# Attention in full fp32 on halves of TensorE, with no hi/lo splits and TensorE in program order

## Chip, core and metric

The kernel runs on one core of one Trainium2 chip. The metric is the device time of one execution in microseconds. Before the change the median of three runs is 1240.89 us (1240.23 to 1241.39).

## Reference

Block-causal attention over 8 batches and 8 heads (576 positions, head size 64, blocks of 64) is followed by a bilinear feed-forward layer on the 4608 x 512 result.

```python
def _attn_ref(q, k, v):
    scores = (1.0 / np.sqrt(D)) * np.matmul(q, k.transpose(0, 1, 3, 2))
    mask = pos[:, None] // 64 >= pos[None, :] // 64
    scores = np.where(mask, scores, -1e9)
    scores = scores - np.max(scores, axis=-1, keepdims=True)
    attn = np.exp(scores)
    attn = attn / (np.sum(attn, axis=-1, keepdims=True) + 1e-09)
    return np.matmul(attn, v).astype(np.float32)

x = attn_out.transpose(0, 2, 1, 3).reshape(B * S, H * D)      # 4608 x 512
return ((x @ w_a) * (x @ w_b)) @ w_out                         # 512 -> 1536 -> 512
```

All inputs are fp32, and so are the results. q and k are drawn about four times as wide as v.

## The kernel before, in words

**Two phases.** The first phase does the attention of 64 heads, and mixed into it the feed-forward layer for four of twelve blocks of 128 hidden units ("moe" below; helper `mm3`, line 223). The second phase (lines 746 and 792) does the other eight blocks. It starts when the matmuls of `first_pass` and its tail (`o_ahead`, line 583) are through. The change touches nothing in it.

**Number formats.** The chip takes fp32 in two ways here. An `F32` matmul is shown in the trace as two MATMUL records (two passes, each with a weight load of its own). An `F32R` matmul is one record. For F32R the kernel splits an operand into a high part and a remainder (`split`, lines 112 and 115) and adds the products. The first `NATIVE = 8` heads use F32 directly, with 64 rows of the array (head size 64); the other 56 use splits. For those, q and k are split (`split_q`, `split_k`), the parts are copied by DMA so that high and low lie in the two 64-row halves of one tile (`spread`), and one F32R matmul over 128 rows sums two products. v is split into 64 + 64 columns (`split_v`), and the attention matrix into `ah` and `al` (line 478).

**One head.** There are four tiles t = 0..3 of 128 query rows, which see 192, 320, 448 and 512 keys, and a "side" tile of 128 rows by 128 keys for the first and last block. The generators are `softmax` (scores on PE; row maxima with `top` on DVE, line 404; exponentials with `exps` on ACT, line 407; sums and reciprocal `rc`; multiplication by `rc` on POOL, line 451), `turn` (14 transposes of 128 x 128 on PE, line 474; copies `ah` out of PSUM on ACT, line 476) and `values` (products with v into `av`, copied to `xf`). PSUM has three score buffers, two buffers `tp` for the transposes and one `av`.

**Slots.** The loop at the end goes through 66 slots. In slot s, head s starts, head s-1 is transposed and head s-2 gets its values; the table `SLOT` says in which order the generators step, and how many moe matmuls come after a step (its third number, 36 in a full slot). Moe matmuls start at 10.2 slots (`MOE_FROM`) with 31 to a slot, and with 36 from slot 18 on. Until slot 11 the loop also emits the conversion of the weights (`convert_w`, five steps a slot on DVE and ACT). `KEEP` adds empty matmuls in the first slots.

**Order.** `PE_ORDER` is empty: the scheduler of the language orders the instructions of every engine, PE too, by its own estimate of when they can run.

Of the kernel before, what the change touches and what calls it, by code (L numbers as in the profile page):

```python
# [9 lines left out]
F32 = mybir.dt.float32  # L10
# [22 lines left out]
PE_ORDER = []  # L33
NATIVE = 8
SPARE = 8
WARM = 9
KEEP = {(0,3):4,(1,0):2,(1,1):2,(1,2):2,(1,3):6}
# [17 lines left out]
def attention_then_bilinear_ffn(  # L55
# [11 lines left out]
    B, H, D, S = kT.shape  # L67
    SQ = qT.shape[3]
# [216 lines left out]
    c0 = [min(max(P * c - BLK, 0), S - BLK - 256) for c in range(NCH)]  # L285
    W = S - BLK
    SIDE, SIDE_T = 3, 1
    SC = slice(P * SIDE_T, P * SIDE_T + BLK), slice(P * SIDE_T + BLK, P * (SIDE_T + 1))
    NE = 2
# [15 lines left out]
    if WARM:  # L305
        z = apool.tile([P, NCH, W], F32R, tag="al", name="z")[:, 0]
        nc.vector.memset(f32(z), 0.0)
        ps = ps_mm.tile([P, 512], F32, tag="mm", name="warm")
        for k in range(WARM):
            nc.tensor.matmul(ps, z[:, :P], z, start=True, stop=True)  # L310
# [4 lines left out]
    pairs = {}  # L315

    def load_pair(p):

        b, h = divmod(2 * p, H)
        n = f"{b}_{h}"  # L320
        if 2 * p < NATIVE:
            qp = apool.tile([P, 1, SQ], F32, tag="q2", name=f"qp{n}", bufs=3)
            kp = apool.tile([P, 2, S], F32, tag="k2", name=f"kp{n}", bufs=3)
        else:
            qp = apool.tile([P, 2, SQ], F32, tag="qp", name=f"qp{n}", bufs=2)
            kp = apool.tile([P, 2, S], F32, tag="kp", name=f"kp{n}", bufs=2)
        nc.sync.dma_start(kp[:, 1], kT[b, h:h + 2].rearrange("h d s -> (h d) s"))
        nc.sync.dma_start(qp[:, 0], qT[b, h:h + 2].rearrange("h d s -> (h d) s"))
        pairs[p] = qp, kp
        for j in range(2):  # L330
            heads[2 * p + j] = {"q": qp[j * D:(j + 1) * D, 0], "k": kp[j * D:(j + 1) * D, 1]}
# [5 lines left out]

    def split_q(p):
        qp = pairs[p][0]
        if 2 * p < NATIVE:  # L340
            nc.vector.tensor_scalar_mul(qp[:, 0], qp[:, 0], SCALE)
            return
        nc.scalar.mul(qp[:, 1].bitcast(F32R), qp[:, 0], SCALE)
        behind_of(nc.vector.scalar_tensor_tensor(
            qp[:, 0], qp[:, 0], SCALE, qp[:, 1], op0=ALU.mult, op1=ALU.subtract), "rc")

    def split_k(p):
        kp = pairs[p][1]
        if 2 * p >= NATIVE:
            nc.scalar.copy(kp[:, 0].bitcast(F32R), kp[:, 1])  # L350
            nc.gpsimd.tensor_tensor(kp[:, 1], kp[:, 1], kp[:, 0], op=ALU.subtract)

    def spread(i):

        if i < NATIVE:
            return
        qp, kp = pairs[i // 2]
        n = "%d_%d" % divmod(i, H)
        own = slice(i % 2 * D, (i % 2 + 1) * D)
        q2 = heads[i]["q2"] = apool.tile([P, SQ], F32R, tag="q2", name=f"q2{n}", bufs=3)  # L360
        k2 = heads[i]["k2"] = apool.tile([P, 2, S], F32R, tag="k2", name=f"k2{n}", bufs=3)
        for j in range(2):
            part_ = slice(j * D, (j + 1) * D)
            nc.sync.dma_start(f32(q2[part_]), qp[own, 1 - j])
            nc.sync.dma_start(f32(k2[part_]), kp[own])

    def split_v(i):

        if i < NATIVE:
            return  # L370
        n = "%d_%d" % divmod(i, H)
        vr = heads[i]["vr"]
        v2 = heads[i]["v2"] = apool.tile([P, NCH + 1, 2, D], F32R, tag="v2", name=f"v2{n}", bufs=2)
        split(v2[:, :, 0], v2[:, :, 1], vr, nc.scalar, nc.gpsimd)
# [5 lines left out]
    def softmax(i):  # L380

        t, n = heads[i], "%d_%d" % divmod(i, H)
        native = i < NATIVE
        if native:
            qm, ks = t["q"], [t["k"]]
        else:
            qm, ks = t["q2"], [t["k2"][:, j] for j in range(2)]
# [7 lines left out]
        def scores(t, ps):  # L395
            w = nk[t] if native else max(nk[t], 256)
            for i, kk in enumerate(ks):
                mark = nc.tensor.matmul(  # L398
                    ps[:, :w], qm[:, q0[t]:q0[t] + P], kk[:, :w], start=(i == 0), stop=(i == len(ks) - 1)
                )  # L400
            return mark
# [7 lines left out]

        if i < SPARE:  # L410
            ps = ps_mm.tile([P, 512], F32, tag="mm", name=f"sl{n}")
        else:
            ps = ps_sc.tile([P, 512], F32, tag="sc", name=f"sl{n}")

        p1 = ps_sc.tile([P, 512], F32, tag="sc", name=f"s1{n}")
        side = p1[:, nk[1]:nk[1] + P]
        for j, kk in enumerate(ks):
            nc.tensor.matmul(side, qm[:, q0[NT]:], ends(kk), start=(j == 0), stop=(j == len(ks) - 1))  # L418
        nc.vector.memset(side[:BLK, BLK:], NEG)
        nc.vector.memset(side[BLK:, :BLK], NEG)  # L420
        mark = scores(LAST, ps)
        top(NT, side)
        top(LAST, ps)

# [3 lines left out]
            nb[BLK:], two[BLK:, None, :].to_broadcast([P - BLK, 2, 2]), axis=AX.X, op=ALU.min)  # L428
        exps(NT, e_s, side, nb[:, 1:])
        exps(LAST, es[LAST], ps, nb[:, :1])  # L430
        yield mark
        for t in range(LAST):
            ps = p1 if t == 1 else ps_sc.tile([P, 512], F32, tag="sc", name=f"s{t}{n}")
            mark = scores(t, ps)

            nc.vector.memset(ps[:BLK, nk[t] - BLK:nk[t]], NEG)
            top(t, ps[:, :nk[t]])
            exps(t, es[t][:, :nk[t]], ps[:, :nk[t]], nm[:, t:t + 1])
            if t < LAST - 1 or not native:
                yield mark  # L440
        ins = nc.vector.tensor_reduce(rc, sm, axis=AX.X, op=ALU.add)
        if not native:
            behind_of(ins, "nb")
# [9 lines left out]
        if native:  # L453
            yield mark

    def turn(i):
# [4 lines left out]
        native = i < NATIVE  # L461
        ah = apool.tile([P, NCH, W], F32 if native else F32R, tag="ah", name=f"ah{n}")
        al = None if native else apool.tile([P, NCH, W], F32R, tag="al", name=f"al{n}")
        heads[i]["a"] = ah, al
        for t in range(LAST, -1, -1):
# [11 lines left out]
            def lower(tp=tp, m=m, cols=cols):  # L477
                return nc.vector.tensor_tensor(al[:, :m, cols], tp[:, :m], f32(ah[:, :m, cols]), op=ALU.subtract)  # L478

            if t == SIDE_T and not native:  # L480
                yield mark
                behind_of(lower(), "rc")
                continue
            if not native:
                ins = lower()
                if t == 0:
                    behind_of(ins, "rc")
            yield mark

    def values(i):  # L490
# [4 lines left out]
        ah, al = t["a"]  # L495
# [6 lines left out]
        if i < NATIVE:  # L502
            an, vr = ah, t["vr"]
            av0 = ps_t.tile([P, 512], F32, tag="tp", name=f"av0{n}", bufs=2)
            nc.tensor.matmul(av0[:D, :BLK], vr[:, NCH], an[:, SIDE, SC[0]], start=True, stop=True)
            nc.scalar.copy(xo[:, :BLK], av0[:D, :BLK])

            at = [0] + [P * c - BLK for c in range(1, NCH)] + [W - BLK, W]
            for g in range(NCH + 1):
                cols = slice(at[g], at[g + 1])  # L510
                last = min(g, NCH - 1)
                for c in range(last + 1):
                    mark = nc.tensor.matmul(  # L513
                        av[:D, cols], vr[:, c], an[:, c, cols], start=(c == 0), stop=(c == last and g < NCH)
                    )
                if g == 2:
                    yield mark
            nc.tensor.matmul(av[:D, W - BLK:], vr[:, NCH], an[:, SIDE, SC[1]], start=False, stop=True)
            nc.scalar.copy(xo[:, BLK:], av[:D])
        else:  # L520
            v2 = t["v2"]
            for c in range(NCH):
                mark = nc.tensor.matmul(av[:, c0[c]:], v2[:, c], ah[:, c, c0[c]:], start=(c == 0), stop=False)  # L523
            yield mark
            av0 = ps_t.tile([P, 512], F32, tag="tp", name=f"av0{n}", bufs=2)
            for j, a in enumerate((ah, al)):
                nc.tensor.matmul(av0[:, :P], v2[:, NCH], a[:, SIDE, SIDE_T * P:][:, :P], start=(j == 0), stop=(j == 1))
            for c in range(NCH - 1, -1, -1):
                mark = nc.tensor.matmul(av[:, c0[c]:], v2[:, c], al[:, c, c0[c]:], start=False, stop=(c == 0))  # L529

            lo = apool.tile([D, S + BLK], F32, tag="avlo", name=f"avlo{n}", bufs=1)
            lo0, lo = lo[:, :P], lo[:, P:]
            nc.scalar.copy(lo0, av0[D:, :P])
            nc.vector.tensor_tensor(xo[:, :BLK], av0[:D, :BLK], lo0[:, :BLK], op=ALU.add)
# [73 lines left out]
    for p in range(2):  # L608
        load_pair(p)
        split_q(p)  # L610
# [329 lines left out]
```

## Time and profile before

| | |
|---|---|
| median of 3 runs | 1240.89 us |
| span of the profiled execution | 1238.6 us |
| first moe matmul | 95.23 us after the span's start |
| first matmul of the second phase | 677.04 us |
| PE matmul records, busy | 7849, 1222.5 us |
| DVE, ACT, POOL busy | 974.6, 706.6, 415.5 us |

The profiled execution has no wall time of its own beside its span; the 2.3 us between the span and the median lie around the span. PE's busy time overlaps from record to record, since matmuls are pipelined; what a matmul costs is read from the distance between the starts of neighbouring records.

### The profile page before, as it was taken

How to read it: one execution, taken by the hardware profiler on the slowest of the kernel's cores; microseconds unless marked ns; L12 is line 12 of the kernel's file. 1: busy time of each engine (PE TensorE's matmuls, PEld its weight loads, DVE VectorE, ACT ScalarE, POOL GpSimd, SP SyncE). 2: the span in 40 equal slices, each digit the busy share in tenths (PEclk: the TensorE clock that was granted, in tenths of full speed). 3: DMA queues.
4: the chain of work that ended last, by engine and by line, in shares of the span. 5: the costliest groups of instructions: out<-in, count | busy, mean ns of one | idle time of the engine just before them, and what ended most of it. 6: DMA issues, size and time to landing. Idle time of an engine off the chain costs nothing.

```text
span 1238.6 us, 23305 instructions
## 1 busy us (share of the span) xinstructions
PE 1222.5 (99%) x7849; PEld 1170.0 (94%) x7849; DVE 974.6 (79%) x2485; ACT 706.6 (57%) x1770; POOL 415.5 (34%) x583
## 2 busy tenths in 40 slices
PE   9989999999999999999999999999999999999998
PEld 5668999999999999999999999999999999999998
DVE  6898888777877778778889988878878677677654
ACT  5788878788788887888756345334334222222210
POOL 4467666566665666656500022022021000000000
PEclk8999999999999999999999999999999999999999
DMA  6468766767667776676234266266298344144131
GB/s 222 140 185 224 199 161 166 188 170 185 164 172 181 176 185 164 169 182 158 71 121 150 92 152 167 82 157 162 76 258 272 122 141 127 40 140 126 28 103 64
DMA packets 86583, 187.13 MB, mean 151 GB/s; under 512 B 11200, under 2 KB 46016, under 8 KB 86464
## 3 DMA queue, kind: packets, MB, share of 16 engines
q1 hardware_dynamic: 74944, 166.76, 48.6%
q0 software_dynamic: 6912, 9.44, 4.8%
q10 hardware_dynamic: 4608, 9.44, 2.2%
q8 instruction: 63, 1.03, 0.3%
q14 instruction: 56, 0.46, 0.1%
HBM read 87.03 MB, written 47.19 MB: 108 GB/s over the span
## 4 chain that ended last, share of the span: by engine, by line
PE 85%; DVE 7%; DMA 3%; ACT 2%; issue 1%; POOL 1%; SPq 0%; ACTq 0%; DVEq 0%; POOLq 0%
PE pso_z L792 15%; PE ps L223 12%; PE psx_z L746 8%; PE psw_z L746 8%; PE psv_z L746 8%; PE tp L474 8%; PE pso L223 5%; PE s L398 5%; PE psy_z L746 4%; PE av L523 3%; PE av L529 3%; PE sl L398 2%; PE av L513 2%; PE s L418 1%; DMA kp<-kT 1%
## 5 line engine op out<-in xcount | busy, mean ns | idle before, releaser
L223 PE MATMUL ps<-xh,wab 128*128 128x288 f32 x1024 | 240.7, 303 | 0.0
L792 PE MATMUL pso_z<-h_z,wo 128*128 128x384 f32 x1152 | 203.1, 334 | 0.0
L451 POOL TENSOR_SCALAR e<-e,rc 128x512 f32<-128x512 f32 (+3 forms) x256 | 154.6, 616 | 137.7 <-DVE rc L448 122.7
L792 PEld LDWEIGHTS pso_z<-h_z,wo 128*128 128x128 f32 x1152 | 199.9, 188 | 0.4 <-ACT h_z L112 0.3
L223 PEld LDWEIGHTS ps<-xh,wab 128*128 128x128 f32 x1024 | 172.0, 188 | 3.4
L223 PE MATMUL ps<-xl,wab 128*128 128x288 f32 x512 | 154.2, 301 | 0.0
L478 DVE TENSOR_TENSOR al<-tp,ah 128x512 fp32r<-128x512 f32 x224 | 131.7, 607 | 27.7 <-ACT ah L476 26.7
L112 ACT CAST h_z<-u_z 128x384 fp32r<-128x384 f32 x96 | 49.3, 514 | 180.0 <-DVE u_z L771 163.4
L476 ACT CAST ah<-tp 128x512 fp32r<-128x512 f32 x224 | 116.7, 533 | 53.0 <-PE tp L474 49.5
L474 PE MATMUL tp<-ident,e 128*128 128x128 f32 x832 | 135.9, 278 | 5.0 <-DVE al L478 1.8
L855 POOL DMA_DIRECT2D part<-pt x48 | 42.8, 1012 | 291.4 <-ACT pt L854 291.3
L474 PEld LDWEIGHTS tp<-ident,e 128*128 128x128 f32 x832 | 100.5, 141 | 20.0 <-issue 6.7
L223 PE MATMUL pso<-hh,wo 128*128 128x288 f32 x480 | 118.6, 308 | 0.0
L746 PE MATMUL psx_z<-xh,wab 128*128 128x384 f32 x384 | 116.4, 338 | 1.8 <-DVE u_z L764 1.8
L407 ACT ACTIVATE e<-s,nm 128x192 f32<-128x192 f32 (+2 forms) x192 | 101.8, 530 | 28.3 <-DVE nm L404 18.4
L746 PE MATMUL psw_z<-xh,wab 128*128 128x384 f32 x384 | 116.2, 338 | 0.0
L746 PE MATMUL psv_z<-xh,wab 128*128 128x384 f32 x384 | 116.2, 338 | 0.0
L404 DVE TENSOR_REDUCE nm<-s 128x1 f32<-128x128 f32 (+3 forms) x256 | 109.8, 430 | 2.1
L223 PEld LDWEIGHTS ps<-xl,wab 128*128 128x128 f32 x512 | 96.4, 188 | 3.6 <-POOL xl L115 0.2
L398 PE MATMUL s<-k,q 128*128 128x256 f32 x336 | 80.7, 321 | 2.1 <-ACT e_s L407 1.6
L223 PEld LDWEIGHTS pso<-hh,wo 128*128 128x128 f32 x480 | 81.5, 189 | 1.2
L115 POOL TENSOR_TENSOR v<-vr,v 128x320 fp32r<-128x320 f32 x56 | 49.7, 887 | 91.6 <-ACT v L112 78.6
(147 smaller groups left out, 2857.9 us busy)
## 6 DMA issues: line engine op xcount, KB each, us to landing
k<-kp SPq DMA_DIRECT2D x112, 288.0 KB, 4.2
xr<-xd SPq DMA_DIRECT2D x48, 384.0 KB, 4.0
q<-qp SPq DMA_DIRECT2D x112, 160.0 KB, 2.5
raww<-wab SPq DMA_DIRECT2D x24, 512.0 KB, 3.8
qp<-qT SPq DMA_DIRECT2D x32, 320.0 KB, 3.2
vr<-vm SPq DMA_DIRECT2D x64, 160.0 KB, 3.3
kp<-kT SPq DMA_DIRECT2D x32, 288.0 KB, 3.3
xd<-xf ACTq DMA_DIRECT2D x32, 288.0 KB, 4.8
```

Of the source, the lines that this page charges most:

```text
L112: nc.scalar.copy(hi, src)
L115: return lo_eng.tensor_tensor(lo, src, f32(hi), op=ALU.subtract)
L223: mm = nc.tensor.matmul(ps, w_, d_, start=(i == 0), stop=(i == n - 1))
L398: mark = nc.tensor.matmul(ps[:, :w], qm[:, q0[t]:q0[t] + P], kk[:, :w], start=(i == 0), stop=(i == len(ks) - 1))
L404: nc.vector.tensor_reduce(nm[:, t:t + 1], view, axis=AX.X, op=ALU.max, negate=True)
L407: nc.scalar.activation(out, view, AF.Exp, bias=bias, accum_out=sm[:, t, :1])
L451: nc.gpsimd.tensor_scalar(ev, ev, rc[:, t:t + 1], 1.0, op0=ALU.mult, op1=ALU.mult)
L474: mark = nc.tensor.transpose(tp[:, c], src, ident)
L476: nc.scalar.copy(ah[:, :m, cols], tp[:, :m])
L478: return nc.vector.tensor_tensor(al[:, :m, cols], tp[:, :m], f32(ah[:, :m, cols]), op=ALU.subtract)
L746: nc.tensor.matmul(ps, wt[:, i, iw], j[:, ix], start=start and kp == 0 and i == 0 and j is xh, stop=kp == KP - 1 and i == 1, skip_group_ch ...
L792: nc.tensor.matmul(ps, wt[:, a, osl], b, start=i == 0, stop=i == 3 * len(fs) - 1)
```

## The change

All 64 heads use F32. The host gives q and k twice, so that 64 channels lie in both halves of the 128 rows. Scores of tiles 1 and 3 use rows 0 to 63, those of tiles 0, 2 and the side tile rows 64 to 127. Values go into two halves of `av`: columns 0 to 63 of the array hold the outputs for the first 384 positions, columns 64 to 127 those for the last 192. `spread`, the splits and `al` are gone. There are three sets of exponential buffers for two, `SLOT` and `KEEP` have other entries, q is scaled on POOL, and PE runs the first phase in program order; the other engines are still ordered by the scheduler.

```diff
-PE_ORDER = []
-NATIVE = 8
-SPARE = 8
+PE_ORDER = ["PE"]
-KEEP = {(0,3):4,(1,0):2,(1,1):2,(1,2):2,(1,3):6}
+KEEP = {(0, 0): 6, (1, 0): 3, (1, 1): 3, (1, 2): 2, (1, 3): 2, (1, 4): 2}
...
+    CUT = 320
-    NE = 2
+    NE = 3
...
+    def scale_q(i):
+        qq = heads[i]["q"]
+        (nc.vector if i < 2 else nc.gpsimd).tensor_scalar(qq, qq, SCALE, 1.0, op0=ALU.mult, op1=ALU.mult)
...
-    def split_q(p):
...
-    def spread(i):
...
-    def split_v(i):
...
+        def scores(out, t, half, keys):
+            rows = slice(half * D, (half + 1) * D)
+            return nc.tensor.matmul(out, qm[rows, q0[t]:q0[t] + P], keys[rows], start=True, stop=True)
...
+        ps = [ps_sc.tile([P, 512], F32, tag="sc", name=f"s{t}{n}") for t in (1, 0)][::-1]
+        side = ps[0][:, nk[0]:nk[0] + P]
+        scores(side, NT, 1, ends(kk))
+        scores(ps[1][:, :nk[1]], 1, 0, kk[:, :nk[1]])
+        mark = scores(ps[0][:, :nk[0]], 0, 1, kk[:, :nk[0]])
...
+        ps += [ps_sc.tile([P, 512], F32, tag="sc", name=f"s{t}{n}") for t in (LAST, 2)][::-1]
+        scores(ps[LAST], LAST, 0, kk[:, :nk[LAST]])
+        mark = scores(ps[2][:, :nk[2]], 2, 1, kk[:, :nk[2]])
...
-        al = None if native else apool.tile([P, NCH, W], F32R, tag="al", name=f"al{n}")
...
+        for c in range(NCH):
+            a0 = max(P * c - BLK, 0)
+            if a0 < CUT:
+                part_(slice(D), slice(BLK + a0, BLK + CUT), vr[:, c], ah[:, c, a0:CUT], c == 0, False)
+            else:
+                part_(slice(D), slice(BLK), vr[:, NCH], ah[:, SIDE, SC[0]], False, True)
+            part_(slice(D, P), slice(W - CUT), vr[:, c], ah[:, c, CUT:], c == 0, False)
+        mark = part_(slice(D, P), slice(W - CUT - BLK, W - CUT), vr[:, NCH], ah[:, SIDE, SC[1]], False, True)
+        nc.scalar.copy(xo[:, :BLK + CUT], av[:D, :BLK + CUT])
+        nc.vector.tensor_copy(xo[:, BLK + CUT:], av[D:, :W - CUT])
...
-    SLOT = [(S_, 0, 3), (S_, -1, 0), (T_, -2, 4), (S_, 0, 4), (V_, -2, 3), (S_, 0, 3),
-            (T_, -1, 4), (V_, -2, 3), (S_, 0, 3), (T_, -1, 5), (T_, -1, 4)]
+    SLOT = [(S_, 0, 0), (V_, -2, 7), (S_, -1, 0), (T_, -1, 6), (S_, 0, 7), (T_, -1, 5), (T_, -1, 5), (T_, -1, 6)]
```

**PE, the start of a steady slot.** Here batch 3's head 4 starts (`s13_4` holds tile 1 and the side tile, `sl3_4` tile 3, `s03_4` tile 0), and head 2 gets its values; `x2` is the split's two matmuls. Before:

```order
L418 MATMUL s13_4_3981<-k23_4_3768,q23_4_3767 128x128 x2
L398 MATMUL sl3_4_3980<-k23_4_3768,q23_4_3767 128x512 x2
L223 MATMUL ps0_2_0_1_3997<-xh2_0_0_2651,wab1_80 128x288
...
L398 MATMUL s03_4_4022<-k23_4_3768,q23_4_3767 128x256 x2
...
L523 MATMUL av3_2_4033<-ah3_2_3897,v23_2_3854 128x512
L523 MATMUL av3_2_4033<-ah3_2_3897,v23_2_3854 128x448
L523 MATMUL av3_2_4033<-ah3_2_3897,v23_2_3854 128x320
L523 MATMUL av3_2_4033<-ah3_2_3897,v23_2_3854 128x256
L398 MATMUL s13_4_3981<-k23_4_3768,q23_4_3767 128x320 x2
```

The same place now, one head later (head 5 starts, head 3 gets its values; each row is one F32 matmul of two passes; `128x` rows are scores, `64x` rows values):

```order
L350 MATMUL s03_5_3600<-k3_5_3190,q3_5_3191 128x128
L350 MATMUL s13_5_3599<-k3_5_3190,q3_5_3191 128x320
L350 MATMUL s03_5_3600<-k3_5_3190,q3_5_3191 128x192
L430 MATMUL av3_3_3613<-ah3_3_3515,vr3_3_3328 64x320
L430 MATMUL av3_3_3613<-ah3_3_3515,vr3_3_3328 64x192
L430 MATMUL av3_3_3613<-ah3_3_3515,vr3_3_3328 64x256
...
L430 MATMUL av3_3_3613<-ah3_3_3515,vr3_3_3328 64x128
...
L430 MATMUL av3_3_3613<-ah3_3_3515,vr3_3_3328 64x64
...
L222 MATMUL ps1_2_0_2_3636<-xh2_0_0_2287,wab2_82 128x288
```

Scores and values, which lay between moe matmuls on all 128 rows and columns, now stand in two blocks one behind the other: three scores on half the rows, then nine value matmuls on half the columns, then seven moe matmuls.

**ACT, from the exponentials of a head to the copies of the transposes.** `e` tiles are exponentials, `ah` the copies out of `tp`. Before, tile 3 and the side tile come first, and the copy of the next head's tile 3 stands between the exponentials:

```order
L407 ACTIVATE e0_s_115,sm0_113<-s13_4_3981,nb3_4_3979 128x128
L407 ACTIVATE e0_3_109,sm0_113<-sl3_4_3980,nb3_4_3979 128x512
L407 ACTIVATE e0_0_106,sm0_113<-s03_4_4022,nm3_4_3977 128x192
L247 COPY a_2_0_1_4039<-ps0_2_0_1_3997 128x288
L476 CAST ah3_3_4056<-tp3_3_3_4058 128x4x128
L407 ACTIVATE e0_1_107,sm0_113<-s13_4_3981,nm3_4_3977 128x320
```

Now, for head 4 and the transposes of head 3:

```order
L413 COPY ah3_3_3515<-tp3_3_3_3516 128x4x128
L246 COPY a_2_0_1_3527<-ps0_2_0_1_3499 128x288
L356 ACTIVATE e1_3_119,sm1_123<-s33_4_3531,nb3_4_3468 128x512
L356 ACTIVATE e1_s_125,sm1_123<-s03_4_3470,nb3_4_3468 128x128
L356 ACTIVATE e1_2_118,sm1_123<-s23_4_3532,nm3_4_3466 128x448
L413 COPY ah3_3_3515<-tp3_3_2_3550 128x4x128
L111 CAST hh_2_0_1_3562<-hf_2_0_1_3560 128x288
L413 COPY ah3_3_3515<-tp3_3_1_3568 128x4x128
```

The copy of tile 2's transposes (`tp3_3_2`) now stands behind three exponentials of the head whose second score block has just run on PE.

**PE, around that place now.** Between the second score block (`s33_4`, `s23_4`) and the transposes of tile 0 (`tp3_3_0`) stand 17 moe matmuls and the transposes of tiles 2 and 1:

```order
L350 MATMUL s33_4_3531<-k3_4_3053,q3_4_3054 128x512
L350 MATMUL s23_4_3532<-k3_4_3053,q3_4_3054 128x448
L222 MATMUL ps1_2_0_1_3529<-xl2_0_0_2288,wab1_80 128x288
...
L411 MATMUL tp3_3_2_3550<-ident_101,e0_2_108 128x128 x4
...
L411 MATMUL tp3_3_1_3568<-ident_101,e0_1_107 128x128 x3
L411 MATMUL tp3_3_1_3568<-ident_101,e0_s_115 128x128
...
L411 MATMUL tp3_3_0_3579<-ident_101,e0_0_106 128x128 x2
```

The transposes of tile 0 take the `tp` buffer that tile 2 had, so they wait for the copy of `tp3_3_2` shown on ACT.

183 lines of the change are left out of this document (37 added, 146 removed).

## Prediction

> **What bounds the kernel now.** I read the page first (busy shares, the chain), then five stretches of the span, then the start times of single matmuls on PE. The page's rows on the span, on PE, on its granted clock, and on the chain:
>
> ```profile
> span 1238.6 us, 23305 instructions
> PE 1222.5 (99%) x7849; PEld 1170.0 (94%) x7849; DVE 974.6 (79%) x2485; ACT 706.6 (57%) x1770; POOL 415.5 (34%) x583
> PEclk8999999999999999999999999999999999999999
> PE 85%; DVE 7%; DMA 3%; ACT 2%; issue 1%; POOL 1%; SPq 0%; ACTq 0%; DVEq 0%; POOLq 0%
> ```
>
> PE is the bound from end to end. The span by stages (busy time of PE, PE's weight loads, DVE, ACT and POOL, then the clock): up to the first moe matmul, the slots with 31 moe matmuls, those with 36, the tail, the second phase.
>
> ```profile
> 0.00:95.23 95.23, 87.74 (x510) 60.10 (x510) 79.37 (x227) 69.97 (x189) 48.98 (x71) 0.93 0.60 182
> 95.23:168.50 73.27, 72.50 (x511) 67.72 (x510) 62.36 (x196) 61.78 (x174) 47.35 (x67) 1.00 0.80 203
> 168.50:606.50 438.00, 436.90 (x3154) 419.51 (x3152) 348.58 (x1106) 351.34 (x990) 267.40 (x384) 1.00 0.68 168
> 606.50:677.00 70.50, 69.18 (x514) 67.86 (x514) 62.70 (x157) 42.06 (x95) 8.99 (x14) 1.00 0.38 123
> 677.00:1238.60 561.60, 556.22 (x3170) 554.77 (x3168) 421.61 (x803) 181.47 (x327) 42.77 (x48) 1.00 0.45 129
> ```
>
> From 95 us on PE has no gap worth having, while DVE and ACT stand at 80%. So the work taken from DVE, ACT and POOL (splits, `al`, sums of halves) is worth nothing there by itself; what counts is PE's time per head. Rows of the timeline (start, length) for the side tile's scores of heads 18 and 63, for one slot from its start to the next, and of the chain for a run of moe matmuls:
>
> ```profile
> 168.37 0.34 PE L418 MATMUL s<-k,q 128*128 128x128 f32 x2
> 432.15 0.34 PE L418 MATMUL s<-k,q 128*128 128x128 f32 x2
> 441.68 0.34 PE L418 MATMUL s<-k,q 128*128 128x128 f32 x2
> 606.31 0.33 PE L418 MATMUL s<-k,q 128*128 128x128 f32 x2
> 624.54 2.26 PE ps L223 x17
> 677.04 0.34 PE L746 MATMUL psy_z<-xh,wab 128*128 128x384 f32 x1
> ```
>
> A moe matmul takes 2.26/17 = 0.133 us, 36 of them 4.79. The slot from 432.15 lasts 9.53, so a split head costs PE 4.74 us; over 45 slots the mean is (606.31 - 168.37)/45 = 9.73, or 4.94. Over the whole stretch 95.23 to 677.04 there are 64 x 36 = 2304 moe matmuls (306.4 us) and about 55 heads in 581.8 us: 5.01 us a head, with every wait.
>
> **PE's time per head after.** The first eight heads already do scores in F32 on 64 rows, so the trace has the prices. Rows of the timeline from the first 15 us and around 41 and 67 us:
>
> ```profile
> 5.88 1.02 PE L398 MATMUL sl<-kp,qp 64*128 64x512 f32 x2
> 6.74 1.24 PE L398 MATMUL s<-kp,qp 64*128 64x192 f32 x4
> 7.90 0.96 PE L648 MATMUL keep<-z 128*128 128x512 f32 x3
> 8.80 0.69 PE L398 MATMUL sl<-kp,qp 64*128 64x512 f32 x1
> 8.86 0.80 PE L398 MATMUL s<-kp,qp 64*128 64x320 f32 x2
> 9.33 0.59 PE L398 MATMUL sl<-kp,qp 64*128 64x512 f32 x1
> 9.85 0.96 PE L648 MATMUL keep<-z 128*128 128x512 f32 x3
> 12.12 2.12 PE L648 MATMUL keep<-z 128*128 128x512 f32 x8
> 14.16 0.64 PE L398 MATMUL s<-kp,qp 64*128 64x448 f32 x1
> 67.65 0.28 PE L518 MATMUL av<-ah,vr 128*64 128x64 f32 x2
> 67.86 0.98 PE L474 MATMUL tp<-ident,e 128*128 128x128 f32 x7
> 68.69 0.27 PE L474 MATMUL tp<-ident,e_s 128*128 128x128 f32 x1
> ```
>
> - *Streaming.* 512 columns, both passes: 6.74 - 5.88 = 0.86 us, 1.68 ns a column.
> - *Halves of the rows do run side by side.* Head 1's 512 columns start at 8.80 and head 0's 320, on the other 64 rows, at 8.86; both are through when `keep` starts at 9.85. One behind the other they would take 1.40.
> - *A change of shape costs.* The 512 columns from 8.80 to 9.85 take 1.05, not 0.86: 0.10 until the second pass (9.33 - 8.80 = 0.53, not 0.43: first weights not hidden) and 0.09 on leaving. Three `keep` from 7.90 to 8.80 take 0.90, eight from 12.12 to 14.16 take 2.04: 0.228 each, which leaves 0.22 for weights after the return (about 0.11) and for entering (about 0.11). A block on half the array so costs about 0.41 beyond its streaming. From half the columns to all (67.65 to 67.86, less two passes of 64) it is 0.09 as well.
>
> The first score block: side 128 and tile 0's 192 on one half, tile 1's 320 on the other, 320 x 1.68 = 0.54 each; with entry 0.11, weights 0.11, and 0.06 for weights that both halves want at once, 0.82. The values: 768 columns in one half, 832 in the other, 832 x 1.68 = 1.40; with 0.09 to change, 0.05 for 64 columns of weights, 0.04 between nine pairs, 1.58; return 0.09 + 0.11 = 0.20. The second block: 512 x 1.68 = 0.86, with 0.22 to enter 1.08; return 0.20. Fourteen transposes, seven of which with the side one from 67.86 to 68.69 give 0.83/7 = 0.119, of which the first carries 0.06 of weights: 0.109 each, 1.52. Sum: 0.82 + 1.58 + 0.20 + 1.08 + 0.20 + 1.52 = 5.40 us against 4.74. Streaming is 0.4 us shorter than the split's, the changes of shape cost about 1.0.
>
> Whether halves of the *columns* run side by side no row shows: values in the first heads use one column half alone. Bounds: 1.40 if they do, 1600 x 1.68 = 2.69 if not. I take 1.40, since the row halves are the nearest rows. The Trainium skill (TensorE: Matmul & The Clock Gate, Part 3, "Measured speedup vs the span model") has three column tiles at 2.38 times the speed of one; by it the values stay near 1.40 too.
>
> **A new wait.** PE is in order now, and the transposes of tile 0 need the `tp` buffer that ACT empties after three exponentials of the next head. Rows of PE, DVE and ACT for the same work before (PE's 512 columns at F32R end 0.21 after the second pass starts at 432.61, which the merged row holds):
>
> ```profile
> 432.33 0.67 PE L398 MATMUL sl<-k,q 128*128 128x512 f32 x2
> 433.04 0.69 DVE L404 TENSOR_REDUCE nm<-sl 128x1 f32<-128x512 f32 x1
> 433.96 0.15 DVE L426 TENSOR_REDUCE nb<-nm 64x2 f32<-64x2 f32 x1
> 434.12 0.15 DVE L427 TENSOR_REDUCE nb<-nm 64x2 f32<-64x4 f32 x1
> 434.37 0.37 ACT L407 ACTIVATE e_s<-s,nb 128x128 f32<-128x128 f32 x1 [0.35 <-DVE nb L427]
> 434.73 0.68 ACT L407 ACTIVATE e<-sl,nb 128x512 f32<-128x512 f32 x1
> 435.30 0.20 ACT L407 ACTIVATION_READ_ACCUMULATOR e<-sl,nb 128x1 f32 x1
> 437.21 0.59 ACT L476 CAST ah<-tp 128x512 fp32r<-128x512 f32 x1
> L407 ACT ACTIVATE e<-s,nm 128x448 f32<-128x448 f32 x20 | 12.7, 636 | 2.0 <-DVE nm L404 1.7
> ```
>
> From the end of the columns: maximum 0.2 + 0.7, `nb` 0.35, to ACT 0.1, exponentials 0.67 (tile 3), 0.36 (side, 434.37 to 434.73), 0.63 (tile 2), copy 0.59, to PE 0.1: 3.7 us. PE itself is there after the return 0.2, 17 moe matmuls 2.26, transposes 0.88: 3.3 us. So it waits 0.4 us a slot (0 if ACT's hops are shorter, 1.0 if ACT puts another copy in between), and six moe matmuls and the next head's scores wait behind it. The other waits are covered: tile 3's probabilities need exponentials (3.0), `rc` 0.6 and POOL, and are due 8 us after the same point. That makes 5.8 us a head; 5.4 and 6.4 are its ends.
>
> **The first 95 us.** Without moe matmuls a slot is that loop: second block 1.08, wait 3.7, tile 0 0.22, first block 0.82, values 1.58 and return 0.20, tile 3 0.44: 8.0 us. The conversions of weights add work on ACT in the same slots, of which I put half into the loop, 0.6:
>
> ```profile
> L142 ACT ACTIVATE sw<-sw,shift 128x512 int32<-128x512 int32 x8 | 5.8, 729 | 0.0
> L112 ACT CAST wab<-xw 128x512 fp32r<-128x512 f32 x5 | 3.1, 621 | 2.2 <-DVE xw L151 2.2
> ```
>
> Ten slots of 8.6 (short slot 0 and the part of slot 10 before the first moe matmul cancel) after 5.9 us of start put the first moe matmul at 92 to 96; I take 94, no gain worth naming over 95.23. Ends: 85 with slots of 7.9, 105 if PE's gaps lower its clock, as the 0.93 of that stage shows happens. DVE's 79 us of that stage stay (without q's splits, with copies out of `av`), so it can't be far below 85.
>
> **Sum.** Loads of q and k grow, but the four DMAs of `spread` per head go; PE waits for none. DVE, ACT and POOL work removed: nothing, covered by PE. After: 94 + 306.4 + 54.3 heads x 5.8 (314.9; one head more than before is nearly through at the first moe matmul) + second phase 561.6 = 1277 us of span. Before: 95.2 + 581.8 + 561.6 = 1238.6. The median lies 2.3 us above that span, so I predict 1279 us; 1248 to 1323 with the ends of wait and start.
>
> **Rivals.**
> 1. *Column halves go half in step.* If PE issues matmuls strictly in program order, the second pass of one half holds up the other: stepping the nine pairs through gives 1.82 us of values in place of 1.40, 0.42 x (54.3 + 9) = 27 us more, 1306. Against it: in the rows above head 0's two passes (8.86) both start before head 1's second (9.33), which stands first in the program. In the Trainium skill (TensorE: Matmul & The Clock Gate, Part 3, "The mechanism") matmuls start and end strictly in program order. For row halves the trace contradicts that; for column halves no row here decides.
> 2. *Column halves don't run side by side*, so this half of the change doesn't do what it says: 1.29 x 63.3 = 82 us more, 1361. For it: no row shows them together. Against: the row halves do.
> 3. *Faster.* The changes of shape and their weights hide behind the neighbouring moe matmuls (as weights hide within one shape: 5.88 to 6.74 shows none), and with them the wait of 0.4. They are 1.4 us of 5.8; if two thirds vanish, 0.93 x 54.3 = 50 us, 1229. It turns faster when a head costs less than 276.6/54.3 = 5.09 us, 0.7 below mine. For it: 0.27 us a head of today's 5.01 are waits on splits that go. Against: each change of shape in the rows above costs 0.09 to 0.22.
>
> **Chances.** Forecast 0.63; half in step 0.12; not side by side 0.09; faster 0.13; about as before 0.03. A measurement tells 0.2%, 2.5 us, from nothing. All but the last two are slower: 0.84, same 0.03, faster 0.13. For the range I go down to 1236, which leaves out the larger part of the faster case (0.10), and up to 1330, which leaves out columns one by one (0.09).
>
> **What would show it.** In the profile after: side-tile rows 10.4 to 10.7 us apart in full slots (9.73 now); score rows of both halves starting within 0.1 us of each other, value rows of both column halves too (if a value block spans 1.5 us, rival 1 and 2 fall; 1.9 or 2.8 names them); PE idle before `tp` on ACT `ah`, 20 us in total; the first moe matmul at 94; the second phase 561 to 562 us long. I am wrong if the slot comes out below 9.9: then the changes of shape were priced too high; or if waits other than that for `ah` appear on PE in order.

## Result and the profile after

| | before | after |
|---|---|---|
| median | 1240.74 us (1240.23 to 1241.39) | 1290.76 us (1288.89 to 1291.4) |
| span of the profiled execution | 1238.6 us | 1288.4 us (its time: 1290.17) |
| first moe matmul, start of the second phase | 95.23, 677.04 us | 108.86, 726.72 us |

The changed kernel is slower: ratio 1.0405, 95% interval 1.039 to 1.042, 50 us. All times are those of fast runs; of the paced kernel below, whose fourth run at 1706 us was slow, the median is that of the other three (1284.67 to 1289.6). From the page after: the span, the busy shares, TensorE's clock in 40 slices and the chain that ended last, by engine.

```profile
span 1288.4 us, 22792 instructions
PE 1237.9 (96%) x8187; PEld 1111.6 (86%) x8187; DVE 806.6 (63%) x2071; ACT 633.8 (49%) x1594; POOL 355.1 (28%) x565
PEclk8889999999999999999999999999999999999999
PE 77%; ACT 11%; DVE 8%; issue 1%; DMA 1%; POOL 1%; SPq 0%; POOLq 0%; DVEq 0%; ACTq 0%
```

The work went from DVE (974.6 to 806.6 us), ACT and POOL as the diff says, and bought nothing: PE still ends the span, and on the chain ACT now has 11% where it had 2%. By stages (busy PE, its weight loads, DVE, ACT, POOL, then the clock):

```profile
0.00:108.86 108.86, 76.12 (x425) 47.24 (x426) 83.56 (x238) 68.08 (x183) 52.87 (x89) 0.86 0.54 176
108.86:186.42 77.56, 73.11 (x551) 59.43 (x549) 35.35 (x131) 48.80 (x143) 35.75 (x60) 1.00 0.33 105
186.42:646.71 460.29, 452.46 (x3433) 374.42 (x3432) 204.66 (x748) 289.39 (x836) 210.93 (x352) 1.00 0.32 102
646.71:726.72 80.01, 79.68 (x615) 75.44 (x615) 62.15 (x154) 46.73 (x110) 12.59 (x19) 1.00 0.35 111
726.72:1288.40 561.68, 556.54 (x3170) 555.09 (x3168) 420.85 (x802) 180.79 (x324) 43.00 (x48) 1.00 0.46 129
```

The span grew by 49.8 us: 13.6 up to the first moe matmul, 36.1 between it and the second phase (617.9 for 581.8), 0.1 in the second phase. In the first stage PE is busy for 76 of 109 us, where it was for 88 of 95. PE's waits over the whole run, us in total, times, the longest:

```profile
PE tp L411 <- POOL e L393: 19.9, 10, 5.1
PE tp L411 <- ACT ah L413: 16.3, 53, 2.5
```

The ten on POOL are all in the first stage, and so are 4.5 us of the wait on `ah`. The other 11.7 us of it, in 48 waits behind the first moe matmul, are in the main the wait for tile 0's transposes, once a slot; the view counts them from the modelled end of the matmul before, so they come out shorter than by the distance between starts. One full slot on PE, from the timeline (start, length with the pipeline's tail, operation; merged rows count passes):

```profile
448.29 0.81 PE L350 MATMUL s<-k,q 64*128 64x128 f32 x6
449.03 1.68 PE L430 MATMUL av<-ah,vr 128*64 128x320 f32 x18
450.64 0.40 PE L222 MATMUL pso<-hh,wo 128*128 128x288 f32 x1
450.87 0.29 PE L222 MATMUL pso<-hl,wo 128*128 128x288 f32 x1
...
452.63 0.42 PE L222 MATMUL pso<-hh,wo 128*128 128x288 f32 x2
452.99 1.12 PE L350 MATMUL s<-k,q 64*128 64x512 f32 x4
454.04 0.40 PE L222 MATMUL pso<-hl,wo 128*128 128x288 f32 x1
...
457.13 0.29 PE L222 MATMUL pso<-hh,wo 128*128 128x288 f32 x1
457.59 0.41 PE L411 MATMUL tp<-ident,e 128*128 128x128 f32 x2 [0.16 <-ACT ah L413]
...
458.72 0.54 PE L350 MATMUL s<-k,q 64*128 64x128 f32 x3
```

The slot lasts 458.72 - 448.29 = 10.43 us, against 9.53 before. The values' 1600 columns take 450.64 - 449.03 = 1.61 us, where one column half alone would take 2.69 by 1.68 ns a column. A moe matmul is followed by the next after 0.133 us; the first one after a block in halves takes 0.23 (450.64 to 450.87), so the return costs 0.10; two moe matmuls and the entry take 0.36 (452.63 to 452.99), so the entry costs 0.09. The second scores take 454.04 - 452.99 = 1.05 us for 512 columns that stream in 0.86, so another 0.19 lies inside a block that stands alone. Tile 0's transposes come 0.46 after the last moe matmul, 0.33 too late. What they wait for, on ACT:

```profile
455.22 0.69 ACT L356 ACTIVATE e<-s,nb 128x512 f32<-128x512 f32 x1 [1.82 <-DVE nb L377]
...
456.25 0.64 ACT L356 ACTIVATE e<-s,nm 128x448 f32<-128x448 f32 x1
...
456.85 0.59 ACT L413 COPY ah<-tp 128x512 f32<-128x512 f32 x1
```

The copy of tile 2 stands behind the exponentials of the next head, ends at 457.44, and gives its buffer to tile 0.

The first stage has ten slots without moe matmuls. The side scores of head 0 and head 10:

```profile
5.59 0.62 PE L350 MATMUL s<-k,q 64*128 64x128 f32 x3
...
106.10 0.81 PE L350 MATMUL s<-k,q 64*128 64x128 f32 x6
```

They last (106.10 - 5.59)/10 = 10.05 us each on the mean, and the blocks of one head are some 5.1 us of PE's time at full clock (the slot above without its wait, returns and moe matmuls). Pieces of the chain between two such slots (start, length, what):

```profile
59.82 0.66 PE tp L411 x4
60.47 2.00 PE s L350 x3
...
69.94 0.94 POOL e L393
...
70.93 1.12 PE tp L411 x4
```

From one tile 3 to the next it is 11.1 us: second scores behind the transposes, maxima, exponentials, sums, POOL's division, transposes. On DVE, steps of the weight conversion stand between the links. Here two of them (L114, L148) stand between the first sum and the reciprocal that POOL waits for:

```profile
67.32 0.14 DVE L385 TENSOR_REDUCE rc<-sm 128x5 f32<-128x10 f32 x1
67.35 0.67 DVE L114 TENSOR_TENSOR wab<-xw,wab 128x512 fp32r<-128x512 f32 x1
...
68.50 0.69 DVE L148 SCALAR_TENSOR_TENSOR sw<-raww,sw 128x512 int32<-128x512 int32 x1
...
69.62 0.15 DVE L390 RECIPROCAL rc<-rc 128x5 f32<-128x5 f32 x1
```

The copy of the second column half out of `av`, which the change gives to DVE, stands there too (69.23, 0.36 us). Part of the loop runs at half clock: PE was idle for 4.3 us ahead of 59.82 and for 2.6 us ahead of 70.93, and the granted clock is 0.50 from 60.5 to 62.5 and from 70.9 to 72.1. The second scores at 60.47 take 2.00 us, where the full slot has 1.05; the four transposes at 70.93 take 1.12, those at 59.82, still at full clock, 0.66.

### The profile page after: what moved, and what is told of

It is laid out like the page before. It is cut to its first block, busy times and chain, and to the rows that moved or that the text cites. A ratio compares the mean times of both kernels' runs of the same rounds, so it can differ in the third digit from the quotient of the medians.

```text
span 1288.4 us, 22792 instructions
## 1 busy us (share of the span) xinstructions
PE 1237.9 (96%) x8187; PEld 1111.6 (86%) x8187; DVE 806.6 (63%) x2071; ACT 633.8 (49%) x1594; POOL 355.1 (28%) x565
## 4 chain that ended last, share of the span: by engine, by line
PE 77%; ACT 11%; DVE 8%; issue 1%; DMA 1%; POOL 1%; SPq 0%; POOLq 0%; DVEq 0%; ACTq 0%
PE pso_z L688 14%; PE ps L222 10%; PE s L350 9%; PE psx_z L642 8%; PE psw_z L642 8%; PE psv_z L642 8%; PE av L430 7%; ACT e L356 6%; PE tp L411 5%; PE pso L222 5%; PE psy_z L642 4%; DVE nm L353 3%; ACT ah L413 2%; ACT e_s L356 1%; POOL e L393 1%
## 5 line engine op out<-in xcount | busy, mean ns | idle before, releaser
L222 PE MATMUL ps<-xh,wab 128*128 128x288 f32 x1024 | 232.0, 306 | 0.0
L353 DVE TENSOR_REDUCE nm<-s 128x1 f32<-128x320 f32 (+4 forms) x320 | 156.2, 490 | 104.8 <-PE s L350 97.1
L411 PE MATMUL tp<-ident,e 128*128 128x128 f32 x832 | 138.3, 282 | 37.1 <-POOL e L393 19.9
L222 PE MATMUL ps<-xl,wab 128*128 128x288 f32 x512 | 160.0, 313 | 0.0
L413 ACT COPY ah<-tp 128x512 f32<-128x512 f32 (+1 forms) x256 | 132.5, 550 | 44.5 <-PE tp L411 43.9
L350 PE MATMUL s<-k,q 64*128 64x128 f32 (+4 forms) x640 | 131.9, 488 | 4.0 <-ACT e L356 4.0
L356 ACT ACTIVATE e<-s,nm 128x320 f32<-128x320 f32 (+2 forms) x192 | 101.3, 528 | 66.1 <-DVE nm L353 64.7
L222 PEld LDWEIGHTS ps<-xl,wab 128*128 128x128 f32 x512 | 96.4, 188 | 27.9 <-issue 27.8
L430 PEld LDWEIGHTS av<-ah,vr 128*64 128x64 f32 x1152 | 86.9, 137 | 31.9 <-ACT ah L413 6.5
L430 PE MATMUL av<-ah,vr 128*64 128x192 f32 (+4 forms) x1152 | 108.8, 325 | 2.8 <-ACT ah L413 2.8
L222 PE MATMUL pso<-hh,wo 128*128 128x288 f32 x480 | 111.0, 305 | 0.0
L356 ACT ACTIVATE e<-s,nb 128x512 f32<-128x512 f32 x64 | 44.1, 689 | 96.6 <-DVE nb L377 96.6
```

What stands on the lines that cost most here:

```text
L222: mm = nc.tensor.matmul(ps, w_, d_, start=(i == 0), stop=(i == n - 1))
L350: return nc.tensor.matmul(out, qm[rows, q0[t]:q0[t] + P], keys[rows], start=True, stop=True)
L353: nc.vector.tensor_reduce(nm[:, t:t + 1], view, axis=AX.X, op=ALU.max, negate=True)
L356: nc.scalar.activation(out, view, AF.Exp, bias=bias, accum_out=sm[:, t, :1])
L411: mark = nc.tensor.transpose(tp[:, c], src, ident)
L413: nc.scalar.copy(ah[:, :m, cols], tp[:, :m])
```

## Experiments

Times are medians beside runs of the kernel before on the same chip, and ratios are to that kernel; its own median was between 1239.5 and 1240.7 us in all of them. "First moe" is the start of the first moe matmul in the profiled run.

| run | time | ratio, 95% interval | first moe |
|---|---|---|---|
| changed kernel | 1290.8 | 1.0405 (1.039 to 1.042) | 108.9 |
| no conversion | 1277.2 | 1.0295 (1.0274 to 1.0316) | 94.9 |
| before, no conversion | 1230.4 | 0.9911 (0.9888 to 0.9934) | 83.4 |
| more filler on PE | 1295.3 | 1.044 (1.0416 to 1.0464) | 114.3 |
| paced conversions | 1287.0 | 1.0369 (1.0334 to 1.0403) | 103.8 |
| scheduler's order on PE | 1299.6 | 1.047 (1.0443 to 1.0497) | 109.0 |
| before, PE in program order | 1273.7 | 1.0258 (1.0227 to 1.0289) | 104.5 |
| tile 2 first | 1284.2 | 1.0352 (1.0325 to 1.0378) | 118.0 |
| blocks apart | 1299.8 | 1.048 (1.0456 to 1.0505) | 106.3 |
| paced, tile 2 first from slot 11 | 1268.5 | 1.0216 (1.0186 to 1.0247) | 104.4 |
| the same, blocks together | 1257.3 | 1.0131 (1.0108 to 1.0155) | 105.3 |
| the same from slot 0 on | 1255.7 | 1.0131 (1.0113 to 1.015) | 105.0 |
| before, values in column halves | 1251.2 | 1.0073 (1.005 to 1.0096) | 96.4 |

### The first stage: conversions left out

```diff
+        if not paced:
+            for _ in range(4):
+                yield
+            return raw.bitcast(F32)[:, :, 1], None
```

> The first pass's weights are not put together from their two words: five of a part's six steps on DVE and one of its two on ACT are left out, and the upper word is taken as a number (so the weights are others). Theory A (the conversions, 4.1 us of DVE for each of 12 parts, stand in DVE's order inside the attention chain of the first slots, and set their length): the first stage loses about 10 of its 15 us over the forecast, the first matmul of the first pass starts at 97 to 101 us instead of 108.9, 1279 to 1283 us in all. Theory B (half clock after gaps) and theory C (the chain of one head in a fixed order is that long by itself): it moves by less than 3 us, 1288 to 1291 us.

13.6 us less than the changed kernel, a little more than theory A asked for. Side scores of heads 0 and 10 in this run, and two of PE's waits over the whole of it:

```profile
5.49 0.81 PE L354 MATMUL s<-k,q 64*128 64x128 f32 x5
...
92.09 0.81 PE L354 MATMUL s<-k,q 64*128 64x128 f32 x6
```

```profile
PE tp L415 <- ACT ah L417: 27.1, 52, 2.7
PE tp L415 <- POOL e L397: 1.6, 1, 1.6
```

The slots are 8.66 us long instead of 10.05; the stretch to the second phase (617.7 us) and the rest are as they were. So the conversions cost 1.39 us a slot on the mean. The waits and DVE's order point to the sums: the wait on POOL's division falls from 19.9 to 1.6 us, and 16.4 us of the wait on ACT's copies, where the changed kernel had 4.5, now lie in the first stage. The price isn't even. The second slot, the longest, lasts 16.0 us with the conversions and 10.5 without; in it DVE needs from 13.24 to 17.51 us for the sums and the reciprocal of head 0, with five conversion steps among them, and without them from 12.43 to 13.24. One of two steps on ACT is left out as well, and its share wasn't separated. That alone doesn't say that the change made them cost something; for that the same edit went into the kernel before:

> The kernel before without the conversion of the first pass's weights (upper word taken as the number, as in the changed kernel's run). There it was worth 13.6 us. Theory (the changed order and blocks make DVE's conversions cost, in the kernel before they lie beside PE's work, which is busy for 90% of that stage): 0 to 5 us, 1236 to 1241 us. Rival (the conversions cost the kernel before as much, and the 15 us have another cause): 10 us or more, 1230 us or less.

The rival holds: 10.4 us less there too. The stage up to the first moe matmul, busy time as above:

```profile
0.00:83.44 83.44, 80.70 (x510) 56.17 (x510) 47.52 (x169) 63.94 (x178) 37.64 (x73) 1.00 0.73 226
```

Without conversions the kernel before is bound by PE in its first slots (80.7 of 83.4 us, clock 1.00). The changed one is not: it has less PE work there and still takes 94.9. With conversions the first moe matmul comes 13.6 us later than before, without them 11.4. The conversions are thus a price that both kernels pay, and only some 2 to 3 us of it are new; the larger part is there without them: PE, busy for 71 of the 94.9 us, waits for ACT's copies (the 16.4 us above), where the kernel before, without its conversions, waits 0.6 us for them.

### The first stage: clock, pace, and the place of the second scores

More filler matmuls to hold the clock (in slots 2 to 9, into a PSUM buffer that is free there):

```diff
-KEEP = {..., (1, 4): 2}
+KEEP = {..., (1, 4): 2, **{(s, k): m for s in range(2, 10) for k, m in ((0, 8), (4, 5))}}
```

> Matmuls on a zero tile that nobody reads are added in slots 2 to 9, eight behind the values and five behind tile 1's transposes (0.19 us each at full clock), where PE stands idle for 1 to 4.3 us and then runs passes of 128 columns in 213 ns instead of 107. Theory B (the half clock lengthens the early slots): at full clock scores, values and transposes of some six slots take 1.5 to 2.5 us less each, so 8 to 12 us less: the first-pass matmuls start at 97 to 101 us, 1279 to 1283 us in all. Theory A (DVE's conversions set the slots) and theory C (the chain's latency): a block sooner ready waits for DVE or ACT instead, less than 3 us either way, 1288 to 1294 us.

The clock rose as meant, and the time with it:

```profile
0.00:108.86 108.86, 88.00 (x496) 59.48 (x497) 82.08 (x228) 64.91 (x170) 49.47 (x83) 0.94 0.52 170
```

0.94 in place of 0.86, and the first moe matmul 5.4 us later, so theory B's forecast misses. It doesn't show that the half clock costs nothing: the filler takes PE's time too, about 0.23 us apiece (0.228 by the rows in the prediction, not 0.19), some 24 us for the 104 that were added, and in program order it stands ahead of blocks that may be ready. PE's waits for the other engines in the first stage fell from 31.2 to 20.6 us only. What the clock alone gave back wasn't separated.

Conversions in step with the slots:

```diff
+            else:
+                behind_of(ins, "nb")
+                behind_of(ins, "rc")
...
-            while n_conv < 5 * int(now * CONV_PER_SLOT + CONV0):
+            while n_conv < int(5 * (now * CONV_PER_SLOT + CONV0)):
```

> All conversions stay, but each step is ordered on DVE behind the latest maxima and sums of the attention program that were written ahead of it, one step after each of the slot's blocks, so that they stand in 12 slots instead of 8. Theory (it is the conversions' place in DVE's order that costs the 14 us): half to all of it comes back, first matmul of the first pass at 95 to 102 us, 1277 to 1284 us. Rival (it is their amount, 4.1 us of DVE for each part beside some 3.5 us of a head's own work in slots of 7 to 9 us): at most 3 us come back, 1287 to 1292 us.

Between the two: the first moe matmul is 5.1 us earlier, the median 3.8 us lower. The intervals of the two ratios overlap (1.0334 to 1.0403, and 1.039 to 1.042 for the changed kernel), so the gain in time isn't clear of the noise. This pacing brings back about a third of what the conversions cost; that the rest is their amount, as the rival has it, isn't shown.

Last, from the version with the three blocks together (below): the second scores of head s ahead of tile 3 of head s-1 in the first slots too.

```diff
-        for what, i, m in SLOT if s < 11 else SLOT2:
+        for what, i, m in SLOT2:
```

> As the kernel with the three blocks together (1257.3 us), but in the first slots too: there the second scores of head s now stand ahead of the third tile's transposes of head s-1 instead of behind them. Theory of the loop: in the changed kernel's first slots the transposes of tile 3 wait for a head's second scores, maxima, exponentials, sums and POOL's division, and the next head's second scores stand on PE behind those transposes; one turn of the loop took 11.1 us (59.82 to 70.93) and there is nothing else for PE to run. With the second scores ahead, two heads share a turn, and the slots fall from about 9.1 to what DVE needs with a conversion, 7.5 to 8 us: first matmul of the first pass at 91 to 98 us instead of 105.3, 1243 to 1252 us. Rival (DVE's conversions or ACT's queue set the first slots, not the place of the second scores on PE): slots stay at 9 us, 1254 to 1260 us.

The rival holds, the ratio is the same. PE's waits between 20 and 103 us, first in the version with the three blocks together, then in this run:

```profile
PE tp L414 <- ACT ah L416: 12.5, 9, 1.8
PE tp L414 <- POOL e L396: 6.8, 8, 1.6
```

```profile
PE tp L414 <- ACT ah L416: 10.4, 9, 2.8
PE av L433 <- ACT ah L416: 3.9, 4, 1.2
PE s L353 <- ACT e L359: 3.6, 7, 1.7
...
PE tp L414 <- POOL e L396: 0.2, 1, 0.2
```

The wait on POOL, which the loop explained, is gone (0.2 us for 6.8). In its place PE waits longer on ACT ahead of values and scores (3.9 and 3.6 us, 0.6 each before), and the sum of its waits is 19.7 us where it was 20.5; the values at 72.37 run at a granted clock of 0.52. So the loop that the chain shows was real, but not the only one of its length. Which queue would have to be relieved first is open.

### Program order by itself

The changed kernel with `PE_ORDER = []`:

> The changed kernel with PE's order left to the scheduler. In its order the first score blocks of a head and the large tile of its second block stand ahead of the values and transposes of the heads before, so PE has a block to run while DVE is late. Theory (the conversions cost 14 us only because PE's order is fixed): the first matmul of the first pass starts at 95 to 101 us; the later slots hold the same blocks with 10 changes of shape more in the whole attention stage, 2 us; 1278 to 1286 us. Rival (DVE's amount of work sets the stage, whatever PE's order): first matmul at 106 to 112 us, 1289 to 1296 us.

Neither theory: the first moe matmul stays at 109.0, and the time is 8.8 us worse.

```profile
0.00:108.86 108.86, 89.90 (x383) 52.41 (x383) 71.77 (x210) 60.51 (x163) 42.20 (x76) 0.76 0.48 156
```

PE is busy for 90 us of that stage instead of 76, but at a clock of 0.76, and has less of the program behind it (383 recorded passes against 425). The first moe matmul is no measure of the stage here, since the scheduler puts it ahead of late heads: head 10 starts at 113.09 us where it started at 106.10. The full slots last 10.43 us on the mean in both kernels (heads 12 to 62), so the loss lies in the slots ahead of them. The scheduler also drew the filler matmuls of the first slots to the front; its order and its clock weren't separated. As the kernel stands, program order is a gain of 9 us, all of it in the first dozen slots. For the kernel before it is not (`PE_ORDER = ["PE"]` there):

> The kernel before with PE in program order and nothing else changed. Theory (a fixed order leaves PE waiting at the head of each late block, above all in the first slots, where it was 10 to 14 us in the changed kernel): 1250 to 1262 us. Rival (the order is worth nothing by itself; the loss belongs to the full fp32 heads): 1239 to 1243 us.

33 us worse, more than the theory asked for. 9.3 of them are there at the first moe matmul. The rest is a wait that the kernel before hardly has (1.8 us in 5 waits):

```profile
PE tp L474 <- DVE al L478: 26.8, 22, 2.0
```

The `al` split on DVE reads the `tp` buffer and holds it. The change takes this split away; whether that is enough for PE to stand in program order, no run tells by itself.

### The steady slot: the wait and the changes of shape

Tile 2's transposes ahead of the second scores:

```diff
-(T_, -1, 6), (S_, 0, 7), (T_, -1, 5), (T_, -1, 5), (T_, -1, 6)]
+(T_, -1, 6), (T_, -1, 5), (S_, 0, 7), (T_, -1, 5), (T_, -1, 6)]
```

> Theory: in a full slot of the changed kernel tile 0's transposes start 0.455 us after the last first-pass matmul instead of 0.133, because their buffer is that of tile 2, whose copy stands on ACT behind the three exponentials of the second score block. With tile 2 turned ahead of that block, its copy ends before the exponentials are asked for and the 0.32 us go: about 50 slots x 0.32 = 16 us less, 1275 us against 1290.8, and full slots of 10.12 instead of 10.44. Rival: ACT's queue is only turned round, the exponentials or the copy of tile 1 then stand late, and the wait comes back at the next slot's first transposes or at the scores: slots of 10.35 to 10.5 and 1286 to 1294 us.

```profile
456.47 0.81 PE L350 MATMUL s<-k,q 64*128 64x128 f32 x6
...
466.63 0.65 PE L350 MATMUL s<-k,q 64*128 64x128 f32 x4
```

A full slot takes 10.16 us: 0.27 less, 16 us over 52 slots by their mean of 10.11 against 10.42. The wait is gone as the theory has it. The total falls by 7 only, since the first moe matmul comes at 118.0: in the first slots, one more tile now stands ahead of the second scores in the loop (a reading of the order; no run tests it). With the old order up to slot 10, and paced conversions:

```diff
-        for what, i, m in SLOT:
+        for what, i, m in SLOT if s < 11 else SLOT2:
```

> The paced conversions, and tile 2's transposes ahead of the second score block from slot 11 on only. With that order in every slot the full slots were 0.31 us shorter, but the first pass started 9 us later. Theory (the two terms are independent): the time of the paced kernel alone less 50 x 0.31 = 15 us, so 1262 to 1270 us where the paced kernel is at 1277 to 1284. Rival (the wait for tile 0 returns elsewhere once the first slots are different): within 4 us of the paced kernel.

1268.5 us, 18.5 below the paced kernel, whose three runs spread over 5 us, and 15.4 between the two profiled spans, where 15 were forecast: the terms add up. Next, the price of a change of shape, by one return and one entry more in each slot:

```diff
-    SLOT = [(S_, 0, 0), (V_, -2, 7), ...
+    SLOT = [(S_, 0, 4), (V_, -2, 3), ...
```

> Four of the seven first-pass matmuls that follow the values are put between the first score block and the values, so that each slot has one return to whole-array matmuls and one entry into half-array ones more; no other work changes. Theory (a change of shape costs about 0.20 us for a block of row or column halves, the return 0.10 and the entry 0.09): slots of 10.44 + 0.20 = 10.64 and, in some 50 slots, 10 us more, 1301 us. Rival (the 0.20 belong to the waits on the data ahead of each block, not to the change of shape): nothing added, or something taken away because the values get their copies later, 1285 to 1292 us.

```profile
451.86 0.81 PE L350 MATMUL s<-k,q 64*128 64x128 f32 x6
452.60 0.40 PE L222 MATMUL pso<-hh,wo 128*128 128x288 f32 x1
452.84 0.30 PE L222 MATMUL pso<-hl,wo 128*128 128x288 f32 x1
...
462.50 0.54 PE L350 MATMUL s<-k,q 64*128 64x128 f32 x2
```

The slot takes 10.64, 0.21 more, and the first of the four moe matmuls 0.24. It is 9.0 us in all, with the first moe matmul 2.6 us earlier. And one change less, the second scores right behind the values:

```diff
+    SLOT2 = [(S_, 0, 0), (V_, -2, 0), (S_, -1, 0), (S_, 0, 9), (T_, -1, 7), (T_, -1, 7), (T_, -1, 6), (T_, -1, 7)]
```

> As the kernel with paced conversions and tile 2 first (1268.5 us), but from slot 11 on a head's second score block stands right behind the values, so that first scores, values and second scores are one stretch in half arrays: one return and one entry less in each slot. Theory (a change of shape costs 0.10 back and 0.09 in): about 50 x 0.19 = 10 us less, 1257 to 1261 us, full slots of 9.97. Rival (the second scores then wait for a score buffer that the first block's exponentials still hold, 1 us or more): 1268 us or more, slots of 10.2 and over.

```profile
456.49 0.81 PE L353 MATMUL s<-k,q 64*128 64x128 f32 x6
...
466.40 0.81 PE L353 MATMUL s<-k,q 64*128 64x128 f32 x5
```

9.91 in place of 10.16, and 11.2 us less. One more costs 0.21 us a slot and one less saves 0.25, so a return with an entry is worth 0.2 to 0.25. The Trainium skill (TensorEngine Tiling (Array Packing), Key Properties) says that changing the tiling mode drains TensorE; it gives no price. These slots agree with it, at 0.09 us for the entry and 0.10 for the return.

### The kernel before with column halves in its first eight heads

```diff
-                    mark = nc.tensor.matmul(av[:D, cols], vr[:, c], an[:, c, cols], ...)
+                part_(slice(D), slice(BLK + a0, BLK + CUT), vr[:, c], an[:, c, a0:CUT], c == 0, False)
+                part_(slice(D, P), slice(W - CUT), vr[:, c], an[:, c, CUT:], c == 0, False)
```

> The kernel before, with the values of its first eight heads alone (which it already computes in full fp32) in the changed kernel's two column halves instead of one; nothing else. Theory (two column halves run side by side, 1600 columns in 1.61 us instead of 2.69): 1.08 us less of PE for each of eight heads, and PE is busy for 39 of 43 us in that stage, so 4 to 9 us less, 1232 to 1237 us, which would beat both kernels. Rival (DVE, 89% busy in that stage, sets it): within 2 us of before.

Both theories miss: 10 us slower. The first 140 us of this run, then of the kernel before:

```profile
0.00:140.00 140.00, 119.86 (x635) 84.11 (x635) 113.51 (x330) 98.04 (x263) 72.32 (x104) 0.90 0.63 180
```

```profile
0.00:140.00 140.00, 131.73 (x814) 100.77 (x815) 118.22 (x349) 107.96 (x295) 79.91 (x114) 0.95 0.67 191
```

The second phase starts at 687.47 us instead of 677.04, and those 10.4 us are lost ahead of 140: less PE work, more gaps, a lower clock (0.90 for 0.95). From 140 to 640 PE is as busy as before (497.17 and 497.58 of 500); the profiled run, the slowest of six, loses another 2.7 us in the second phase. Most of it isn't lost where the eight heads with the new values run. Head 10 starts 2.1 us late (96.14 for 94.02), and the slot of head 11 alone, which has moe matmuls already, takes 17.9 us (104.92 to 122.82) instead of 11.1; in it a moe matmul waits 2.2 us for DVE (`hf`), and the granted clock is 0.81. The scheduler also made its order anew; how much is order and how much is lost cover wasn't separated. No version run here with its weights converted beats the kernel before.

## Why the prediction was right in sign and short by 12 us

1290.8 lies above the 1279 and inside the range, which was 94 us wide. Of the 49.8 us by which the span grew, the 36.1 between the first moe matmul and the second phase come as the forecast has them (39.5 said); the 13.6 ahead of it the forecast doesn't have. By its own steps:

- **Second phase.** 561.68 us, as said.
- **The heads between.** Predicted 306.4 + 314.9 = 621.3, measured 617.9, so 5.74 us a head instead of 5.8. In the slot above, from entry to return: first scores 0.74 + 0.09 (0.82 said), values 1.61 + 0.10 (1.58 + 0.20), second scores 0.09 + 1.05 + 0.10 (1.08 + 0.20), wait 0.33 (0.4), transposes 1.53 by what remains of 10.43 - 4.79 (1.52). The 0.09 of leaving, which the sum counts with the return, lies inside the measured 1.61 and 1.05. No term is off by more than 0.07.
- **The new wait.** Right in place and cause (tile 2's copy behind three exponentials); the run with tile 2 first took it away. By starts it is 0.33 us, 17 us over 52 slots, where 20 were said; the page's 16.3 us aren't that number, since 4.5 of them are other waits in the first stage.
- **Column halves.** Rivals 1 and 2 fall: 1.61 us, where 1.9 and 2.8 would have named them; the two halves' first passes start 7 ns apart. In the Trainium skill (TensorE: Matmul & The Clock Gate, Part 3, "The mechanism") matmuls start and end strictly in program order. The trace contradicts that for column halves too: the second matmul of 192 columns starts at 449.41 us, that of 256 columns, which stands ahead of it in the program, at 449.62.
- **Faster.** This rival falls too: the changes of shape are not hidden, as one more and one less of them showed, and a slot of 9.9 came only with other orders, and not even those versions beat the kernel before.
- **The first 95 us.** Here is the miss: 108.9 for 94. The mis-sized term is the slot of the first stage, 8.6 said, 10.05 measured, ten times. Its two parts are told apart by the run without conversions: the loop itself 8.66 where 8.0 was said, 6.6 us in all, and the conversions 1.39 where 0.6 was said, 7.9 in all. The second was priced as half of two steps on ACT; the steps on DVE, which stand between the links of the chain, were left out. The 8.66 still holds half clock (0.91 granted up to the first moe matmul in that run); what that is worth no run separates. Behind the first stage the prediction gained 3.4 us back.
- The prediction named waits other than that for `ah` as a sign against it. They came, all in the first stage: ten on POOL's division, 19.9 us, and 6.8 us on ACT ahead of scores and values. By that sign the account of the first stage was wrong, and only that of the full slots right.

## What to carry to other kernels

Taking work from the engine that bounds a stage helps only until a dependent chain is as long as what is left. Here PE's busy time in the first stage fell from 88 to 76 us, and the stage grew from 95 to 109, with waits and half clock in it. So price the chain with every instruction that its queues hold between the links, not only with its own. Price blocks in a part of the array by their number, not only by their columns: keep them side by side, since each return with its entry cost 0.2 us here, some 10 us over 52 slots. And a fixed order is worth what its waits leave: the same order was a gain of 9 us for one kernel and a loss of 33 for the other.

## What the runs showed of the hardware beyond that

- Two column halves with 768 and 832 columns of work run side by side and without keeping step (1.61 us for 1.40 of the longer one's streaming, with the later matmul of one half starting 0.2 us ahead of the earlier one of the other).
- A higher granted clock came with a later end: 0.94 against 0.86 in the first 108.9 us, and 4.6 us more in all; the filler that raised it takes PE's time as well. The paced kernel reached its first moe matmul 5.1 us sooner than the changed one at about the same clock, 0.88.
